# Converting float64 weights: exponents in a tile of their own, the mantissa in place

## The chip, the cores and the metric

The kernel runs on one core of a Trainium2 chip. The metric is the device time of one execution in microseconds (us): 1454.6, the median of three runs from 1453.09 to 1455.71. PE is TensorE, DVE is VectorE, ACT is ScalarE, POOL is GpSimd; SP, ACT and POOL also issue DMAs.

## The reference

Three steps in a row: an attention between tokens and 32 state rows for 8 batches of 8 heads, a mixture of 8 experts of which every token uses one, and a dense network on all 4352 tokens.

```python
xread = softmax(scale * x @ state.T) @ state      # per batch and head, D = 64
sread = softmax(scale * state @ x.T) @ x
x = concat(xread, sread)                          # 4352 tokens of 512
e = argmax(normalised x @ normalised expert_emb.T / tau)
x = gate * (relu(x @ w1[e]) @ w2[e])              # w1: 8 x 512 x 1024, w2: 8 x 1024 x 512
h = x @ w_in                                      # 512 x 2048
out = (h * clip(h + 3, 0, 6) / 6) @ w_out         # 2048 x 512
```

`w_in` and `w_out` come in as float64: their float32 draws are multiplied by a float64 number. The kernel sees them as pairs of 32-bit words.

## The kernel before

Products that need more precision than one pass gives are made from two parts: a weight or an activation is rounded to a high part (a cast), and a low part is the difference. PE then adds three products (high high, low high, high low).

The attention runs batch by batch. Its results go to DRAM, a routing stage sorts tokens into slots of 128 of one expert, and the slots are worked through in units: five leading slots of the largest expert, then pairs and single slots. An expert's weight pieces (128x512) are loaded to `raw` (L1231, L1234), cast to `wh` on ACT or DVE (L1245) and subtracted to `wl` on DVE or POOL (L1248); PE uses them at L1409 and L1450 (first product, `h_ps`) and L1512 (second product, `y_ps`). Beside the units, blocks of 256 sorted tokens go through the dense network: L1618 (`u_ps`, 12 matmuls for one of 16 pieces of `w_in`), L1622, L1625, L1629, L1632 (the activation and its two parts `gh`, `gl`), and L1653 (`o`, 6 matmuls for one of 16 pieces of `w_out`). The first block needs each of the 32 dense pieces for the first time.

A dense piece is 128x512 float64 numbers, 512 KB, loaded on ACT's queue (L259, L262) into a raw buffer. `Conv` turns it into float32 and then into two parts:

- `cs` (DVE): L271 takes the 11 exponent bits from the top 16 of each number and writes them over the lowest 16 bits; L272 takes the top 20 mantissa bits into a tile of its own, `cv_m`.
- `ct` (ACT): L276 turns the exponent into the bits of a bfloat16 power of two (in its place, the result a whole number of 16 bits); L277 turns the mantissa into 1 + m / 2^20.
- `cd` (DVE): L281 adds the sign bit; L282 adds 16 lower mantissa bits.
- `cp` (POOL or DVE, L286): mantissa times signed power. `ch` (ACT, L293): the high part. `cl` (POOL or DVE, L296): the low part.

The first 14 pieces are converted during the attention and the routing, with two raw buffers and two `cv_m`. The other 18 use as raw buffers the two tiles `yw` and `yh` that later hold tokens, one piece in each at a time, pieces alternating, and rows of a shared pool for `cv_m`.

The order on every engine is set at build time by a planner (`Sched`). Each operation has a cost per engine, an urgency, operations it depends on and buffers that it takes and gives back. The planner keeps an estimated clock for each engine and puts next the operation that can start earliest, corrected by its urgency; where two engines can do an operation it takes the one that ends sooner. A raw buffer (`hr`) is taken by the load and, before, given back by `cp`; the `cv_m` buffer (`hc`) by `cl`. The estimates only set the order: on the chip, engines wait for each other by semaphores.

Of the kernel before, what the change touches and what calls it, by code (L numbers as in the profile page):

```python
# [8 lines left out]
F32 = mybir.dt.float32  # L9
F32R = mybir.dt.float32r  # L10
BF16 = mybir.dt.bfloat16
I32 = mybir.dt.int32
# [8 lines left out]
class Ring:  # L21
    """The buffers of a tag: the times from which those that nothing holds are free."""
# [5 lines left out]
class Hold:  # L28
    """A buffer of a ring, from the operation that takes it to the last of those that read it."""
# [9 lines left out]
class Sched:  # L39
    """Puts operations in the order of the engines' queues: by an estimate of the engines' times, an engine that  # L40
    is free takes the most urgent of the operations whose operands and buffers are there."""
# [9 lines left out]
    def op(self, fn, cost, prio, deps=(), take=(), give=(), dma=0.0, after=None):  # L51
        """After deps have ended, and behind after in the same queue."""
# [18 lines left out]
    def gate(self):  # L71
        """An operation of no engine, that done() does."""
        o = self.op(None, {}, 0.0)
        self.avail.remove(o)
        self.n -= 1
        return o
# [55 lines left out]
def kernel(  # L132
# [33 lines left out]
    # the expert with the most tokens comes first and has at least NT / E of them: the first NL slots are its own  # L166
    NL = -(-NT // (E * 128))
    # behind them, NP pairs of slots of the same expert, that there are always
    NP = -(-(-(-NT // 128) - NL - E) // 2)
    # the slots from NU on are often empty  # L170
    NU = 37
# [9 lines left out]
    # what is kept until the leading slots are done  # L181
# [9 lines left out]
    # A row of xd has its columns (c q a) of 32 in quarters q, for transposes in blocks of 32, the logits behind them:  # L191
    # (q (g (i a) e)), c = 2 g + i, with the products of the heads of g as the second part.
    def quarters(t, g):
        """Columns and logits of g in rows."""
        v = t.rearrange("p (q g w) -> p g q w", q=4, g=2)[:, g]
        return v[:, :, 0:64].rearrange("p q (i a) -> p q i a", i=2), v[:, :, 64:66]
# [25 lines left out]
    # ring buffers  # L222
# [12 lines left out]
    # the attention's end, the leading slots' end, and the end of the slots that may be left out  # L235
# [8 lines left out]
    class Conv:  # L244
        """A piece of a dense weight, rounded to float32, as two float32r parts. A float64 weight comes as its bits:
        exponent and mantissa apart (cs, ct), then the signed power of two, as a bfloat16 in the place of the lowest
        bits, times the mantissa (cd, cp), then the parts (ch, cl)."""
# [16 lines left out]
        def cs(self, pool):  # L264
            self.ma = self.raw
            if self.wide:
                h = self.raw.bitcast(U16).rearrange("p (f w) -> p f w", w=4)
                self.ex, self.low, self.sign = h[:, :, 0], h[:, :, 1], h[:, :, 3]
                self.ma = pool()
                top = self.raw.rearrange("p (f w) -> p f w", w=2)[:, :, 1]  # L270
                DVE.tensor_scalar(self.ex, self.sign, 4, 0x7FF, op0=ALU.logical_shift_right, op1=ALU.bitwise_and)  # L271
                DVE.tensor_scalar(self.ma.bitcast(I32), top, 0xFFFFF, None, op0=ALU.bitwise_and)  # L272

        def ct(self):
            if self.wide:
                ACT.activation(self.ex, self.ex, AF.Relu, bias=ebias[:, 0:1], scale=2.0**7)  # L276
                ACT.activation(self.ma, self.ma.bitcast(I32), AF.Copy, bias=1.0, scale=2.0**-20)  # L277

        def cd(self):
            if self.wide:  # L280
                DVE.scalar_tensor_tensor(self.ex, self.sign, 0x8000, self.ex, op0=ALU.bitwise_and, op1=ALU.bitwise_or)  # L281
                DVE.scalar_tensor_tensor(self.ma, self.low, 2.0**-36, self.ma, op0=ALU.mult, op1=ALU.add)  # L282
# [18 lines left out]
    def convert(n, prio, pool, ma, gate=None, start=0.0):  # L301
        """Takes over a piece: into the buffers of pool, from gate on."""
# [6 lines left out]
        b = op(lambda: c.cs(ma), {"D": 0.67}, prio, [a], [hc])  # L309
        d = op(c.ct, {"A": 1.13}, prio, [b])  # L310
        e = op(c.cd, {"D": 1.2}, prio, [d])
        f = op(*((lambda: c.cp("P"), {"P": 1.225}) if early else (c.cp, {"D": 0.6, "P": 1.225})), prio, [e], (), [hr])
# [1556 lines left out]
```

## Time and profile before

| | |
|---|---|
| median of three runs | 1454.6 us |
| profiled execution, first to last instruction | 1453.4 us |
| PE busy | 1354.7 us, 93% |
| DVE busy | 917.8 us, 63% |
| ACT busy | 645.3 us, 44% |
| POOL busy | 543.1 us, 37% |

The profile tells of one execution. For it the page gives the span of 1453.4 us; the time of that execution from outside isn't given apart, and the runs' median is 1.2 us above the span. The share of busy time is a mean over stages: PE is nearly full from about 450 us on, and has gaps in the attention, the routing, and the stage after it, in which the leading slots end and the first dense block runs.

### The profile page before, as it was taken

Reading aid. Unit: us, or ns where it says so; the run is one execution under the profiler, and the core shown is the slowest. Engines: PE = TensorE matmul, PEld = TensorE weight load, DVE = VectorE, ACT = ScalarE, POOL = GpSimd, SP = SyncE. Lnnn points to the kernel's source line nnn. Section 1 sums busy time; section 2 is a strip of 40 time slices with the busy share of each in tenths; the row PEclk is TensorE's granted clock in tenths of the full one; section 3 lists DMA queues with packets and bytes.
Section 4 is the critical chain, followed back from the end, with each engine's and each line's share of the span. In section 5 each row is a group of like instructions: output and inputs, shape, how many; then the busy total and the mean of one; then the engine's idle time right before and its main releaser. Section 6 shows DMA issues by size and latency. Waiting matters only on the chain. (4 is left out here: it accounts for less than half of the span.)

```text
span 1453.4 us, 25243 instructions
## 1 busy us (share of the span) xinstructions
PE 1354.7 (93%) x8976; PEld 1199.0 (82%) x8976; DVE 917.8 (63%) x2008; ACT 645.3 (44%) x1347; POOL 543.1 (37%) x558
## 2 busy tenths in 40 slices
PE   7896697877799999999999999999999999999997
PEld 6675686766688898989989898999998999899996
DVE  6988888899976555645454544665666675433332
ACT  4785435555643343434444343555544444333332
POOL 5554448566555232524142322244344322200000
PEclk8996689899899999999999999999999999999999
DMA  6643435555564333423243333555455544201000
GB/s 162 175 160 116 148 96 161 156 188 159 157 182 149 94 115 89 136 82 124 90 125 98 108 104 100 154 150 177 152 148 153 174 139 140 74 23 30 15 16 15
DMA packets 151765, 175.64 MB, mean 121 GB/s; under 512 B 43784, under 2 KB 116488, under 8 KB 150608
## 3 DMA queue, kind: packets, MB, share of 16 engines
q1 hardware_dynamic: 128544, 121.19, 28.2%
q0 software_dynamic: 12336, 35.99, 8.2%
q10 hardware_dynamic: 10752, 16.78, 3.6%
q8 instruction: 73, 1.20, 0.4%
q14 instruction: 60, 0.49, 0.1%
HBM read 146.09 MB, written 27.82 MB: 120 GB/s over the span
## 5 line engine op out<-in xcount | busy, mean ns | idle before, releaser
L1618 PE MATMUL u_ps<-yh,wih 128*128 128x256 f32 x1088 | 306.9, 282 | 6.0 <-DVE gl L1632 4.3
L1618 PE MATMUL u_ps<-yh,wil 128*128 128x256 f32 x1088 | 306.8, 282 | 3.1 <-DVE wil L296 3.1
L1618 PE MATMUL u_ps<-yw,wih 128*128 128x256 f32 x1088 | 307.0, 282 | 0.0
L1248 POOL TENSOR_TENSOR wl<-raw,wh 128x512 fp32r<-128x512 f32 x129 | 176.6, 1373 | 274.4 <-ACT wh L1245 127.3
L1625 DVE SCALAR_TENSOR_TENSOR u_ps<-r,u_ps 128x256 f32<-128x256 f32 x272 | 116.2, 427 | 255.0 <-ACT r L1622 240.5
L1622 ACT ACTIVATE r<-u_ps,three 128x256 f32<-128x256 f32 x272 | 129.1, 475 | 305.4 <-PE u_ps L1618 277.2
L1618 PEld LDWEIGHTS u_ps<-yh,wih 128*128 128x128 f32 x1088 | 207.3, 191 | 17.2 <-DVE gl L1632 4.3
L1653 PE MATMUL o<-woh,gh 128*128 128x512 f32 x544 | 217.0, 399 | 2.0 <-DVE yo L1667 1.2
L1653 PE MATMUL o<-wol,gh 128*128 128x512 f32 x544 | 216.4, 398 | 0.0
L1653 PE MATMUL o<-woh,gl 128*128 128x512 f32 x544 | 214.9, 395 | 0.0
L1618 PEld LDWEIGHTS u_ps<-yw,wih 128*128 128x128 f32 x1088 | 206.6, 190 | 8.5
L1618 PEld LDWEIGHTS u_ps<-yh,wil 128*128 128x128 f32 x1088 | 207.5, 191 | 3.3 <-DVE wil L296 3.3
L1512 PE MATMUL y_ps<-wh,hx 128*128 128x512 f32 x512 | 186.3, 403 | 1.3 <-DVE wh L1245 1.3
L1629 ACT CAST gh<-u_ps 128x256 fp32r<-128x256 f32 x272 | 101.2, 372 | 187.9 <-PE o L1653 140.4
L1248 DVE TENSOR_TENSOR wl<-raw,wh 128x512 fp32r<-128x512 f32 x223 | 160.5, 727 | 33.4 <-ACT wh L1245 29.6
L1632 DVE TENSOR_TENSOR gl<-u_ps,gh 128x256 fp32r<-128x256 f32 x272 | 114.4, 421 | 98.0 <-ACT gh L1629 94.3
L1276 POOL DMA_INDIRECT xq<-xd,qidx x128 | 136.1, 1063 | 54.0 <-issue 31.9
L1245 ACT CAST wh<-raw 128x512 fp32r<-128x512 f32 x197 | 120.9, 619 | 73.3 <-PE y_ps L1512 39.8
L1409 PE MATMUL h_ps<-xt,wh 128*128 128x256 f32 x704 | 140.9, 288 | 3.8 <-ACT wh L1245 3.8
L1672 POOL DMA_INDIRECT out_dram<-yo,ix x34 | 35.9, 1057 | 273.3 <-ACT gh L1629 160.0
L1653 PEld LDWEIGHTS o<-woh,gl 128*128 128x128 f32 x544 | 102.6, 189 | 25.2
L1409 PEld LDWEIGHTS h_ps<-xt,wh 128*128 128x128 f32 x704 | 117.6, 197 | 5.7 <-ACT wh L1245 4.2
(312 smaller groups left out, 2474.2 us busy)
## 6 DMA issues: line engine op xcount, KB each, us to landing
raw<-in_moe_w_dram SPq DMA_DIRECT2D x176, 512.0 KB
yl<-ysd SPq DMA_DIRECT2D x136, 64.0 KB
xd<-xr SPq DMA_DIRECT2D x8, 1056.0 KB
ysd<-yt POOLq DMA_DIRECT2D x32, 256.5 KB
xb<-in_x_dram SPq DMA_DIRECT2D x48, 128.0 KB
yw<-in_moe_w_out_dram ACTq DMA_DIRECT2D x9, 512.0 KB
cv_raw<-in_moe_w_in_dram ACTq DMA_DIRECT2D x8, 512.0 KB
yh<-in_moe_w_in_dram ACTq DMA_DIRECT2D x8, 512.0 KB
```

The costliest lines, as they stand in the source:

```text
L1245: copy[e](pc["hi"], box["t"][:, j, :])
L1248: eng[e].tensor_tensor(pc["lo"], box["t"][:, j, :], f32(pc["hi"]), op=ALU.subtract)
L1276: POOL.indirect_dma_start(q[:, j * QW:(j + 1) * QW], None, xd_q, index(qidx[:, j, s:s + 1]))
L1409: PE.matmul(out(f), pc[w][:, (2 * c + f) * 128:(2 * c + f + 1) * 128], u.xt[a][:, 2 * j + c, 256 * hf:256 * hf + 256], start=new and c == ...
L1512: PE.matmul(u.y[i], u.ht[t][:, a, lo + 128 * i:lo + 128 * i + 128], pc[w], start=c == 0 and k == 0, stop=c == KF - 1 and k == 2)
L1618: PE.matmul(p, w, y[:, k, :], start=k == 0 and j == 0, stop=k == KD - 1 and j == 2)
L1622: ACT.activation(q["r"], q["p"], AF.Relu, bias=pool["three"][:, 0:1])
L1625: DVE.scalar_tensor_tensor(q["p"], q["r"], 6.0, q["p"], op0=ALU.min, op1=ALU.mult)
L1629: ACT.copy(q["h"], q["p"])
L1632: DVE.tensor_tensor(q["l"], q["p"], f32(q["h"]), op=ALU.subtract)
L1653: PE.matmul(o["o"][a], g[:, a * 128:(a + 1) * 128], w, start=m == 0 and j == 0, stop=m == KFF - 1 and j == 2)
L1672: POOL.indirect_dma_start(out, bass.IndirectOffsetOnAxis(ap=o["ix"][:, a:a + 1], axis=0), box["t"], None)
```

## The change

The exponents get the tile that the mantissa had (`cv_m`, now used as 512 16-bit numbers side by side), and the mantissa stays in the raw buffer: its mask, its conversion and the lower bits' addition are written in place, 32 bits at every second word. The mask moves from `cs` to `cd`; the conversion becomes a step of its own on ACT (`cu`), and the addition one on DVE (`cm`). So a piece goes DVE, ACT, DVE, ACT, DVE, then `cp`, `ch`, `cl`, where it went DVE, ACT, DVE, `cp`, `ch`, `cl`. The number of instructions of each kind is the same. The raw buffer is now given back by `cl`, and the `cv_m` tile by `cp`. The planner's costs of the steps are new, and with them its order on all engines. Lines move by up to 10: L1245 is L1255 after, L1248 is L1258, L1632 is L1642. The rest of the diff takes comments out.

```diff
         def cs(self, pool):
...
-                self.ex, self.low, self.sign = h[:, :, 0], h[:, :, 1], h[:, :, 3]
-                self.ma = pool()
-                top = self.raw.rearrange("p (f w) -> p f w", w=2)[:, :, 1]
+                self.low, self.sign = h[:, :, 1], h[:, :, 3]
+                self.top = self.raw.rearrange("p (f w) -> p f w", w=2)[:, :, 1]
+                self.ma = self.top.bitcast(F32)
+                self.ex = pool().bitcast(U16)[:, 0:512]
                 DVE.tensor_scalar(self.ex, self.sign, 4, 0x7FF, op0=ALU.logical_shift_right, op1=ALU.bitwise_and)
-                DVE.tensor_scalar(self.ma.bitcast(I32), top, 0xFFFFF, None, op0=ALU.bitwise_and)
         def ct(self):
             if self.wide:
                 ACT.activation(self.ex, self.ex, AF.Relu, bias=ebias[:, 0:1], scale=2.0**7)
-                ACT.activation(self.ma, self.ma.bitcast(I32), AF.Copy, bias=1.0, scale=2.0**-20)
         def cd(self):
             if self.wide:
                 DVE.scalar_tensor_tensor(self.ex, self.sign, 0x8000, self.ex, op0=ALU.bitwise_and, op1=ALU.bitwise_or)
+                DVE.tensor_scalar(self.top, self.top, 0xFFFFF, None, op0=ALU.bitwise_and)
+        def cu(self):
+            if self.wide:
+                ACT.activation(self.ma, self.top, AF.Copy, bias=1.0, scale=2.0**-20)
+        def cm(self):
+            if self.wide:
                 DVE.scalar_tensor_tensor(self.ma, self.low, 2.0**-36, self.ma, op0=ALU.mult, op1=ALU.add)
...
-        b = op(lambda: c.cs(ma), {"D": 0.67}, prio, [a], [hc])
-        d = op(c.ct, {"A": 1.13}, prio, [b])
+        b = op(lambda: c.cs(ma), {"D": 0.6}, prio, [a], [hc])
+        d = op(c.ct, {"A": 0.62}, prio, [b])
         e = op(c.cd, {"D": 1.2}, prio, [d])
-        f = op(*((lambda: c.cp("P"), {"P": 1.225}) if early else (c.cp, {"D": 0.6, "P": 1.225})), prio, [e], (), [hr])
+        e = op(c.cu, {"A": 0.68}, prio, [e])
+        e = op(c.cm, {"D": 0.72}, prio, [e])
+        f = op(*((lambda: c.cp("P"), {"P": 1.225}) if early else (c.cp, {"D": 0.6, "P": 1.225})), prio, [e], (), [hc])
         g = op(c.ch, {"A": 0.52}, prio, [f, home])
-        dense[conv_q[n]] = op(*((lambda: c.cl("P"), {"P": 1.225}) if early else (c.cl, {"D": 0.6, "P": 1.225})), prio, [g], (), [hc])
+        dense[conv_q[n]] = op(*((lambda: c.cl("P"), {"P": 1.225}) if early else (c.cl, {"D": 0.6, "P": 1.225})), prio, [g], (), [hr])
```

Three places show what moves. The first is DVE's order late among the 18 pieces, where one piece takes all its steps; before (L271 and L272 are `cs`, L281 and L282 `cd`, L286 `cp`; the `gl` and `u_ps` rows are the dense block's):

```order
L271 TENSOR_SCALAR yw_4025<-yw_4025 128x512
L272 TENSOR_SCALAR cv_m_4081<-yw_4025 128x512
L1632 TENSOR_TENSOR gl_4070<-u_ps_3965,gh_4069 128x256
L1248 TENSOR_TENSOR wl_4073<-raw_4008,wh_4072 128x512
L1625 SCALAR_TENSOR_TENSOR u_ps_4056<-r_4096,u_ps_4056 128x256
L281 SCALAR_TENSOR_TENSOR yw_4025<-yw_4025 128x512
L282 SCALAR_TENSOR_TENSOR cv_m_4081<-yw_4025,cv_m_4081 128x512
L1248 TENSOR_TENSOR wl_4117<-raw_4040,wh_4116 128x512
L286 TENSOR_TENSOR cv_m_4081<-cv_m_4081,yw_4025 128x512
```

And now (L273 is `cs`, L281 and L282 `cd`, L290 `cm`, L294 `cp`, L304 `cl`; `hx` belongs to a unit):

```order
L273 TENSOR_SCALAR cv_m_4099<-yw_4060 128x512
L304 TENSOR_TENSOR wil2_3177<-yh_3938,wih2_3176 128x512
L281 SCALAR_TENSOR_TENSOR cv_m_4099<-yw_4060,cv_m_4099 128x512
L282 TENSOR_SCALAR yw_4060<-yw_4060 128x512
L1442 SCALAR_TENSOR_TENSOR hx_4134<-h_ps_4046,hx_4134 128x512
L1442 SCALAR_TENSOR_TENSOR hx_4151<-h_ps_4102,hx_4151 128x512
L290 SCALAR_TENSOR_TENSOR yw_4060<-yw_4060 128x512
L294 TENSOR_TENSOR yw_4060<-yw_4060,cv_m_4099 128x512
L273 TENSOR_SCALAR cv_m_4166<-yh_4118 128x512
L304 TENSOR_TENSOR wol2_3175<-yw_4060,woh2_3174 128x512
```

The step `cm` stands between the mask and `cp`, with other work in front of it, a piece's last step stands one row behind the next piece's first, and the two `wl` are gone from DVE's stretch. Next, ACT's order among the same pieces, before (L262 and L259 are loads, L293 is `ch`):

```order
L262 DMA yw_3793<-in_moe2_w_out_dram 128x1024
L293 CAST woh2_3068<-cv_m_3708 128x512
L1354 ACTIVATE l8_3704,gates_83<-l8_3704,nr_3712 128x8
L259 DMA yh_3805<-in_moe2_w_in_dram 128x4x256
L293 CAST wih2_3070<-cv_m_3723 128x512
```

And now (L263 and L260 are the loads, L301 is `ch`):

```order
L301 CAST woh2_3174<-yw_3561 128x512
L301 CAST wih2_3176<-yh_3591 128x512
L1639 CAST gh_3772<-u_ps_3612 128x256
L1364 ACTIVATE l8_3647,gates_83<-l8_3647,nr_3668 128x8
L263 DMA yw_3777<-in_moe2_w_out_dram 128x1024
L260 DMA yh_3780<-in_moe2_w_in_dram 128x4x256
```

The next loads stood in front of the casts of the pieces before them, and stand behind them now. Last, POOL's order late among the 18 pieces, before (L1248 is a `wl`, L1270 a gather of tokens):

```order
L1248 TENSOR_TENSOR wl_4281<-raw_4159,wh_4280 128x512
L1248 TENSOR_TENSOR wl_4301<-raw_4159,wh_4300 128x512
L1248 TENSOR_TENSOR wl_4307<-raw_4230,wh_4306 128x512
L1248 TENSOR_TENSOR wl_4382<-raw_4230,wh_4381 128x512
L1270 DMA xg_4420<-xd_69,gidx1_79 128x528
L286 TENSOR_TENSOR cv_m_4386<-cv_m_4386,yw_4347 128x512
```

And now:

```order
L1258 TENSOR_TENSOR wl_4092<-raw_4041,wh_4091 128x512
L1258 TENSOR_TENSOR wl_4095<-raw_4041,wh_4094 128x512
L1258 TENSOR_TENSOR wl_4160<-raw_4089,wh_4159 128x512
L1258 TENSOR_TENSOR wl_4163<-raw_4089,wh_4162 128x512
L1258 TENSOR_TENSOR wl_4220<-raw_4149,wh_4219 128x512
L1258 TENSOR_TENSOR wl_4259<-raw_4149,wh_4258 128x512
L1258 TENSOR_TENSOR wl_4283<-raw_4203,wh_4282 128x512
L1258 TENSOR_TENSOR wl_4291<-raw_4203,wh_4290 128x512
```

POOL now makes the second parts of both halves of every load here, where DVE made some of them before.

## Rows read from the trace of the kernel before

**Rows 1.** The page: busy us, share of the span and instructions by engine.

```profile
PE 1354.7 (93%) x8976; PEld 1199.0 (82%) x8976; DVE 917.8 (63%) x2008; ACT 645.3 (44%) x1347; POOL 543.1 (37%) x558
```

**Rows 2.** Stretches: length; PE, PEld, DVE, ACT, POOL busy; granted clock; DMA share; GB/s.

```profile
60.00:160.00 100.00, 71.20 (x748) 58.59 (x748) 88.40 (x207) 62.22 (x99) 51.87 (x82) 0.79 0.50 163
...
260.00:410.00 150.00, 116.09 (x617) 99.04 (x618) 144.93 (x233) 85.36 (x155) 93.44 (x71) 0.89 0.53 162
...
450.00:1200.00 750.00, 748.93 (x4816) 676.25 (x4816) 427.01 (x992) 322.37 (x726) 261.51 (x248) 1.00 0.42 126
```

**Rows 3.** PE's waits, 260 to 410 us: total us, times, longest.

```profile
PE y_ps L1512 <- POOL wl L1248: 6.8, 3, 4.1
PE y_ps L1512 <- DVE wl L1248: 5.7, 3, 2.7
PE h_ps L1409 <- DVE wl L1248: 5.3, 2, 3.4
PE h_ps L1409 <- POOL wl L1248: 5.1, 5, 1.6
PE u_ps L1618 <- DVE gl L1632: 4.3, 3, 3.0
PE h_ps L1409 <- ACT wh L1245: 3.8, 2, 2.2
PE u_ps L1618 <- DVE wil L296: 3.1, 1, 3.1
PE u_ps L1618 <- ACT wih L293: 0.8, 1, 0.8
```

**Rows 4.** Tile cv_m: ns least/median/most, first and last start, form.

```profile
L277 ACT ACTIVATE cv_m<-cv_m x32: 629/687/706, 48.8 to 401.5; 128x512 f32<-128x512 int32 x32
...
L293 ACT CAST woh<-cv_m x16: 611/620/623, 208.0 to 404.8; 128x512 fp32r<-128x512 f32 x16
...
L272 DVE TENSOR_SCALAR cv_m<-yw x9: 428/464/3205, 265.6 to 390.2; 128x512 int32<-128x512 int32 x9
...
L282 DVE SCALAR_TENSOR_TENSOR cv_m<-yw,cv_m x9: 706/729/1717, 273.7 to 393.1; 128x512 f32<-128x512 uint16 x9
...
L296 DVE TENSOR_TENSOR wol<-cv_m,woh x9: 671/678/1508, 284.1 to 406.4; 128x512 fp32r<-128x512 f32 x9
...
L286 POOL TENSOR_TENSOR cv_m<-cv_m,yh x3: 1280/1282/1399, 277.6 to 340.2; 128x512 f32<-128x512 f32 x3
L286 DVE TENSOR_TENSOR cv_m<-cv_m,yw x3: 679/679/1773, 311.3 to 383.7; 128x512 f32<-128x512 f32 x3
```

**Rows 5.** Lines L271, L276, L281: the same columns.

```profile
L271 DVE TENSOR_SCALAR yw<-yw x9: 725/746/1839, 265.1 to 389.7; 128x512 uint16<-128x512 uint16 x9
...
L276 ACT ACTIVATE yw<-yw,ebias x9: 1424/1465/1495, 268.1 to 390.5; 128x512 uint16<-128x512 uint16 x9
...
L281 DVE SCALAR_TENSOR_TENSOR yw<-yw x9: 1302/1322/1374, 272.5 to 392.0; 128x512 uint16<-128x512 uint16 x9
```

**Rows 6.** Lines L1245 and L1248: the same columns.

```profile
L1245 DVE CAST wh<-raw x155: 383/427/1533, 212.0 to 1248.4; 128x512 fp32r<-128x512 f32 x155
...
L1248 DVE TENSOR_TENSOR wl<-raw,wh x223: 648/684/4239, 209.2 to 1249.2; 128x512 fp32r<-128x512 f32 x112
L1248 POOL TENSOR_TENSOR wl<-raw,wh x129: 1264/1292/2103, 162.1 to 1247.4; 128x512 fp32r<-128x512 f32 x129
```

**Rows 7.** Timeline, DVE and ACT: start us, length us; idle before it, releaser.

```profile
265.08 0.75 DVE L271 TENSOR_SCALAR yw<-yw 128x512 uint16<-128x512 uint16 x1
...
311.97 0.33 ACTq L262 DMA_DIRECT2D yw<-in_moe_w_out_dram  x1
...
317.48 0.76 DVE L271 TENSOR_SCALAR yw<-yw 128x512 uint16<-128x512 uint16 x1 [0.21 <-DMA yw<-in_moe_w_out_dram]
...
318.27 1.44 ACT L276 ACTIVATE yw<-yw,ebias 128x512 uint16<-128x512 uint16 x1 [2.18 <-DVE yw L271]
...
389.69 0.73 DVE L271 TENSOR_SCALAR yw<-yw 128x512 uint16<-128x512 uint16 x1
```

## The prediction

> **What bounds the kernel now.** I read the busy line first, then busy time and granted clock by stretch, then the waits of the tensor engine in the one stretch that matters, and last the conversion's own instructions. PE is busy 93% of the span [rows 1]; from 450 to 1200 us it is busy 748.9 of 750 us at a granted clock of 1.00 (2.4 GHz), and nothing gained on another engine there can show. The stretch from 260 to 410 us is different: PE has 116.1 busy us in 150 at a mean granted clock of 0.89, while DVE has 144.9, so DVE is idle for 5.1 us of it [rows 2]. PE's waits there add up to 34.9 us: 18.4 end with a DVE instruction (5.7 + 5.3 + 4.3 + 3.1), 11.9 with POOL's `wl`, 4.6 with ACT [rows 3]. So DVE sets the pace of this stretch, everything else queues behind it, and 18 of the 32 weight pieces are converted in it (nine in `yw`, nine in `yh`). The other 14 are converted in the attention before it, which is paced less clearly (60 to 160 us: DVE 88.4 of 100 us, PE 71.2 [rows 2]).
>
> **The change part by part.** A piece now costs DVE L271 0.746 us, L272 0.464, L281 1.322, L282 0.729 [rows 4, 5]: 3.26 us. All read every fourth 16-bit or every second 32-bit element, eight bytes apart. The two that also write at that step are the dear ones: L281 against L282, 1.322 against 0.729, both 512 elements of the same operation; L271 against L272, 0.746 against 0.464. On ACT it is the same: L276, reading and writing 16 bits at eight bytes, takes 1.465 us, L277 0.687.
> - The exponents are now written side by side. The first step (L271) then reads with a step and writes without, like L272: 0.464, at most the old 0.746. The sign step (L281) becomes like L282: 0.729, at most 1.322. Relu on ACT becomes like L277: 0.687, at most 1.465.
> - The mantissa is now written in place: 32 bits at eight bytes. No row of before writes so. From below the nearest rows are those of the same operations with plain writes: mask 0.464, `cu` 0.687, `cm` 0.729, `cp` 0.679 on DVE. From above they are the rows with 16-bit writes at that step: 0.746, 1.465, 1.322, 1.322. I take the lower end: reading 32 or 16 bits at this step costs almost nothing (L282 0.729 against L296 0.678), so the step by itself isn't dear, and the dear rows have one thing more in common, that an element is less than a word.
> - With these, DVE per piece is 0.464 + 0.729 + 0.464 + 0.729 = 2.39 us: 0.87 less, 15.7 us less over the 18 pieces. ACT saves 0.78 per piece, 14 us over the 18; ACT is busy 85.4 of 150 us, so this shortens the chain only.
> - The order changes. Up to the twentieth L1632 on DVE (the dense network's first block is past its last new weight there) DVE is given 10 fewer L1245 (29 to 19), 13 fewer L1248 (35 to 22) and 4 more `cp` (9 to 13). At 0.427, 0.684 and 0.679 [rows 4, 6] that is -4.3 - 8.9 + 2.7 = -10.5 us. POOL takes the 13 `wl` and gives back 4 `cp`: about 13 x 1.292 - 4 x 1.282 = +11.7 us on 93.4 of 150 [rows 2, 4, 6]. That is hidden as long as POOL isn't full.
> - The tensor engine's order puts 18 more L1512 in front of the first L1653, and 24 fewer L1618 and 12 fewer L1409 in front of the sixteenth. The latter 36 come later, where PE is full: one matmul there takes 748.9 / 4816 = 0.156 us [rows 2], so up to 5.6 us; the 18 take 2.8 in front. I book 4.3 us as lost.
> - One step more, and the raw buffer is held to the piece's last step. A buffer's round is now: load, all steps to the multiplication, next load. The nine pieces in `yw` begin from 265.08 to 389.69 us: eight rounds of 15.6 us. From the load's issue to the first step it takes 317.48 - 311.97 = 5.5 us [rows 7]. The new chain from there to the last step is, in order, 0.464 + 0.687 + 0.729 + 0.464 + 0.687 + 0.729 + 0.679 (1.282 on POOL) + 0.620 + 0.678: 5.7 to 6.4 us; with hand-overs of at most 0.1 us between engines, seven of them (L271 ends at 318.24, L276 starts at 318.27 [rows 7]), 6.4 to 7.1. So a round can't be shorter than 11.9 to 12.6 us. By DVE's work: 144.9 / 150 x 15.6 = 15.1 us in a round now, less (15.7 + 10.5) / 9 = 2.9: 12.2. The two bounds lie together, and queues never run without gaps, so I take 13.8 us: 1.8 less in each of nine rounds, 16.2 us.
>
> Sum: -16.2 + 4.3 - 2 (attention: 14 pieces save DVE 12 us there, but PE's waits are spread over many lines, so I count a sixth) = -13.9. The profiled execution's span of 1453.4 us is 1.2 below the median of the runs, 1454.6; I make the difference against the span and add it to the median: 1440.7, taken as 1440. The 18.4 us of waits that end with DVE hold the 13.9.
>
> The row says that reads at eight bytes run at nearly full speed (0.729 against 0.678). The Trainium skill (Vector Engine (DVE) Microarchitecture Reference, 5.2 Measured stream behaviour on trn2) says that a port keeps its rate only with runs of two or more adjacent words that start on an eight-byte boundary; for reads at this step the trace disagrees, and for 32-bit writes no run here shows it. By that rule the in-place writes would be dear, which is the first rival. The Trainium skill (SBUF — State Buffer, Door 1: The DMA port swizzle) speaks of lines of 16 bytes of which two hits are enough; by it the in-place writes would be free, and the reads in the trace agree.
>
> **The rivals.**
> *Writes at eight bytes are dear whatever their width.* For it: every such write in the trace is dear, on two engines. Against it: all of them are 16 bits wide. Then mask, `cu`, `cm` and `cp` take their upper ends: DVE per piece 0.464 + 0.729 + 0.746 + 1.322 = 3.26, nothing saved; 13 `cp` on DVE cost 0.643 more, 8.4 us, against the 10.5 of the order. ACT saves nothing. The chain grows to 0.464 + 0.687 + 0.729 + 0.746 + 1.465 + 1.322 + 1.322 + 0.620 + 0.678 = 8.0, a round with load and hand-overs is 14.2 at least, and with DVE as full as now about 16.2: 0.6 x 9 = 5.4, and 4.3 lost: 1464.
> *The held buffer decides.* The steps get cheaper, but the load of the next piece waits for the last step, which stands in two more queues than the step that now frees it. If that eats the gain, the round stays or grows to 16: 3.6 + 4.3 - 2 = +6, 1460. It turns slower where the round shrinks by less than 0.26 us (2.3 / 9). Against it: in the new order the last step stands one row behind the next piece's first.
> *The waits go to POOL.* DVE gets free, but the pieces' second parts wait on POOL (11.9 us of PE's waits now), which gets 11.7 us more: then the stretch keeps its length and 1455 comes out. Against it: POOL has 56.6 idle us there [rows 2].
>
> **How the numbers follow.** Forecast 0.58, with its own range 1427 to 1450 (round 12.4 to 15); dear writes 0.22; held buffer 0.12; POOL 0.08. No change is within 0.2%, 2.9 us, about what a measurement of this kernel can tell. Faster: 0.54 of the forecast, 0.06 of the others: 0.60. Same: 0.03 + 0.03 + 0.02 + 0.05 = 0.13. Slower: 0.27, nearly all from the first two rivals. The range reaches from 1424 (both bounds of a round met) to 1463, which leaves out about half of the dear writes.
>
> **What would show it.** Right: the sign step near 0.73, Relu near 0.69, mask near 0.46, `cu` near 0.69, `cm` near 0.73; the first steps in `yw` 13 to 14.5 us apart; DVE's busy time in the stretch down by 20 us or more; PE at 99% some 14 us earlier. Wrong: `cu` near 1.46 or `cm` near 1.3 (first rival); rounds of 15.6 us or more with DVE idle, waiting for a load (second); PE's waits for POOL's `wl` well over 12 us (third).

## The result, and the profile after

The changed kernel takes 1470.06 us (median of four runs, 1469.14 to 1471.68) against 1454.51 for the kernel before in the same job: a ratio of 1.0105, 95% interval 1.0091 to 1.012. It is slower by 15.5 us where some 14 us less was forecast, and lies outside the stated range.

The busy line of the page, which answers to [rows 1]:

```profile
PE 1359.6 (93%) x8976; PEld 1200.8 (82%) x8976; DVE 894.1 (61%) x1986; ACT 636.2 (43%) x1358; POOL 544.8 (37%) x569
```

The stretches of [rows 2], with the same columns:

```profile
60.00:160.00 100.00, 70.49 (x745) 56.70 (x744) 84.58 (x191) 57.62 (x99) 52.42 (x81) 0.81 0.48 154
260.00:410.00 150.00, 115.84 (x616) 97.23 (x617) 121.19 (x209) 76.96 (x154) 81.63 (x69) 0.89 0.50 155
450.00:1200.00 750.00, 748.58 (x4769) 675.53 (x4768) 426.64 (x988) 318.95 (x718) 270.65 (x256) 1.00 0.42 126
```

Between 260 and 410 us DVE is busy 23.7 us less than before, about as forecast, and PE no more than before (115.84 against 116.09). From 450 to 1200 us PE is as full as before, yet it gets 47 fewer matmuls through (4769 against 4816), so on average one takes longer.

The conversion's steps after, for the pieces in `yw` and in tile `cv_m` (ns least, median, most; first and last start; form), answering to [rows 4, 5]:

```profile
L277 ACT ACTIVATE cv_m<-cv_m,ebias x32: 706/722/761, 47.4 to 416.7; 128x512 uint16<-128x512 uint16 x32
L273 DVE TENSOR_SCALAR cv_m<-yw x9: 416/428/1415, 274.1 to 407.8; 128x512 uint16<-128x512 uint16 x9
L281 DVE SCALAR_TENSOR_TENSOR cv_m<-yw,cv_m x9: 677/691/731, 278.1 to 409.3; 128x512 uint16<-128x512 uint16 x9
L282 DVE TENSOR_SCALAR yw<-yw x9: 428/431/1407, 278.9 to 410.1; 128x512 int32<-128x512 int32 x9
L286 ACT ACTIVATE yw<-yw x9: 651/677/694, 281.0 to 410.5; 128x512 f32<-128x512 int32 x9
L290 DVE SCALAR_TENSOR_TENSOR yw<-yw x9: 651/682/1669, 282.2 to 412.8; 128x512 f32<-128x512 uint16 x9
```

On DVE these steps came out as priced or a little cheaper: 0.428 + 0.691 + 0.431 + 0.682 = 2.23 us for a piece (2.39 forecast, 3.26 before). On ACT Relu (L277) takes 0.722 us, 0.687 forecast. The 32-bit writes at every eight bytes cost nothing extra: 0.431, 0.677 and 0.682 us against 0.464, 0.687 and 0.729 for the plain writes of before [rows 4]. One step is dearer than its 0.679 us, the product where DVE does it (the same columns):

```profile
L294 DVE TENSOR_TENSOR yh<-yh,cv_m x9: 679/1353/6049, 284.6 to 421.5; 128x512 f32<-128x512 f32 x9
```

The shortest takes what it took before; the longest ran beside POOL, as the last section shows.

The line of L273 also holds the round that the forecast rests on: the first steps in `yw` go from 274.1 to 407.8, so eight rounds of 16.7 us, not 13.8 (before: 15.6). It shows a second thing: the first of these pieces begins 9.0 us later than before (265.08 [rows 7]). Its load is issued that much later, before and after (timeline: start, length):

```profile
259.17 0.33 ACTq L262 DMA_DIRECT2D yw<-in_moe_w_out_dram  x1
```

```profile
268.70 0.34 ACTq L263 DMA_DIRECT2D yw<-in_moe_w_out_dram  x1
```

What DVE waited for between 260 and 425 us, total, times, longest:

```profile
DVE cv_m L273 <- DMA yw<-in_moe_w_out_dram: 9.7, 6, 3.5
DVE hx L1442 <- ACT hx L1438: 4.9, 3, 2.9
DVE cv_m L273 <- DMA ysd<-yt: 4.2, 2, 2.9
DVE cv_m L281 <- ACT cv_m L277: 2.7, 8, 0.8
DVE cv_m L273 <- DMA yh<-in_moe_w_in_dram: 2.5, 3, 1.2
```

DVE, idle for 5.1 us of 150 before, now waits 12.2 us for the pieces' own loads: the sign that was named for the rival "the held buffer decides". PE's own waits from 260 to 410 us, which answer to [rows 3], the longest totals first:

```profile
PE h_ps L1419 <- POOL wl L1258: 7.8, 7, 3.8
PE u_ps L1628 <- DVE gl L1642: 7.3, 3, 4.9
PE h_ps L1419 <- DVE wl L1258: 4.3, 2, 3.6
PE u_ps L1628 <- ACT wih L301: 2.9, 1, 2.9
PE y_ps L1522 <- POOL wl L1258: 2.7, 2, 1.8
PE o L1663 <- DVE wol L304: 2.1, 2, 1.9
```

With the ten shorter rows that follow, 18.3 us end with a DVE instruction (18.4 before), 10.5 with POOL's `wl` (11.9 before) and 5.6 with ACT (4.6 before). DVE has 23.7 us less to do and is idle for 28.8 us of the 150, and PE waits for it as long as before.

How much is lost on the way is read at two places of the dense network's second product (L1653 before, L1663 after), each a pair of matmuls of high parts for one piece of `w_out`: the 24th such pair, in the second block, and the last one (count, ns, first to last start). Before:

```profile
L1653 PE MATMUL o<-woh,gh x2: 391/396/400, 477.4 to 478.1; 128*128 128x512 f32 x2
...
L1653 PE MATMUL o<-woh,gh x2: 398/399/400, 1443.6 to 1444.3; 128*128 128x512 f32 x2
```

After:

```profile
L1663 PE MATMUL o<-woh,gh x2: 391/396/400, 485.5 to 486.2; 128*128 128x512 f32 x2
...
L1663 PE MATMUL o<-woh,gh x2: 397/398/400, 1458.1 to 1458.8; 128*128 128x512 f32 x2
```

8.1 us are gone at the 24th pair, 14.5 at the last. So there are two losses: one before 480 us, and one of 6.4 us spread over the full part. The largest single wait of PE in the first is this (timeline: start, length, engine, line; idle before it and its releaser):

```profile
436.20 0.40 PE L1663 MATMUL o<-woh,gl 128*128 128x512 f32 x1
443.23 0.58 PE L1628 MATMUL u_ps<-yh,wih 128*128 128x256 f32 x1 [6.63 <-DVE gl L1642]
```

DVE is late with `gl` because that stands behind a gate step that waits for POOL. DVE's timeline has that step, and POOL's shows what it waits for queued behind the first block's two output writes:

```profile
440.99 0.15 DVE L1359 TENSOR_SCALAR nr<-nr 128x1 f32<-128x1 f32 x1 [7.31 <-POOL nr L1356]
```

```profile
434.98 1.01 POOL L1682 DMA_INDIRECT out_dram<-yo,ix  x1 [0.30 <-issue]
439.36 0.99 POOL L1682 DMA_INDIRECT out_dram<-yo,ix  x1 [3.37 <-issue]
440.37 1.11 POOL L1356 TENSOR_TENSOR nr<-nr,half 128x1 f32<-128x1 f32 x2
```

Before, the same step (L1346) runs at 415.62, ahead of the first output write (432.42), and PE's longest wait between 400 and 500 us is 2.7. So this wait comes from the order of POOL's queue.

### The profile page after: what moved, and what is told of

It is laid out like the page before. It is cut to its first block, busy times and chain, and to the rows that moved or that the text cites. A ratio compares the mean times of both kernels' runs of the same rounds, so it can differ in the third digit from the quotient of the medians.

```text
span 1468.0 us, 25211 instructions
## 1 busy us (share of the span) xinstructions
PE 1359.6 (93%) x8976; PEld 1200.8 (82%) x8976; DVE 894.1 (61%) x1986; ACT 636.2 (43%) x1358; POOL 544.8 (37%) x569
## 5 line engine op out<-in xcount | busy, mean ns | idle before, releaser
L1628 PE MATMUL u_ps<-yh,wih 128*128 128x256 f32 x1088 | 309.2, 284 | 19.7 <-DVE gl L1642 14.9
L1258 POOL TENSOR_TENSOR wl<-raw,wh 128x512 fp32r<-128x512 f32 x144 | 195.5, 1363 | 310.6 <-ACT wh L1255 166.4
L1628 PE MATMUL u_ps<-yh,wil 128*128 128x256 f32 x1088 | 308.9, 284 | 2.0 <-DVE wil L304 1.3
L1628 PE MATMUL u_ps<-yw,wih 128*128 128x256 f32 x1088 | 308.8, 284 | 0.3 <-DVE yw L1607 0.3
L1632 ACT ACTIVATE r<-u_ps,three 128x256 f32<-128x256 f32 x272 | 129.1, 475 | 306.6 <-PE u_ps L1628 280.4
L1628 PEld LDWEIGHTS u_ps<-yh,wih 128*128 128x128 f32 x1088 | 207.2, 190 | 32.0 <-DVE gl L1642 17.1
L1663 PE MATMUL o<-wol,gh 128*128 128x512 f32 x544 | 215.8, 397 | 2.1 <-DVE wol L304 2.1
L1663 PE MATMUL o<-woh,gh 128*128 128x512 f32 x544 | 215.5, 396 | 1.1 <-ACT woh L301 0.6
L1663 PE MATMUL o<-woh,gl 128*128 128x512 f32 x544 | 215.4, 396 | 0.6 <-DVE gl L1642 0.6
L1628 PEld LDWEIGHTS u_ps<-yw,wih 128*128 128x128 f32 x1088 | 207.3, 191 | 9.3 <-DVE yw L1607 0.9
L1628 PEld LDWEIGHTS u_ps<-yh,wil 128*128 128x128 f32 x1088 | 208.1, 191 | 2.5 <-DVE wil L304 1.6
L1642 DVE TENSOR_TENSOR gl<-u_ps,gh 128x256 fp32r<-128x256 f32 x272 | 114.7, 422 | 101.9 <-ACT gh L1639 100.0
L1258 DVE TENSOR_TENSOR wl<-raw,wh 128x512 fp32r<-128x512 f32 x208 | 150.2, 730 | 33.5 <-ACT wh L1255 29.7
L1255 ACT CAST wh<-raw 128x512 fp32r<-128x512 f32 x206 | 125.9, 619 | 73.7 <-PE y_ps L1522 39.2
L1286 POOL DMA_INDIRECT xq<-xd,qidx x128 | 130.8, 1022 | 51.7 <-issue 33.1
L1663 PEld LDWEIGHTS o<-woh,gl 128*128 128x128 f32 x544 | 102.2, 188 | 24.8 <-DVE gl L1642 1.0
```

What stands on the lines that cost most here:

```text
L1255: copy[e](pc["hi"], box["t"][:, j, :])
L1258: eng[e].tensor_tensor(pc["lo"], box["t"][:, j, :], f32(pc["hi"]), op=ALU.subtract)
L1286: POOL.indirect_dma_start(q[:, j * QW:(j + 1) * QW], None, xd_q, index(qidx[:, j, s:s + 1]))
L1628: PE.matmul(p, w, y[:, k, :], start=k == 0 and j == 0, stop=k == KD - 1 and j == 2)
L1632: ACT.activation(q["r"], q["p"], AF.Relu, bias=pool["three"][:, 0:1])
L1642: DVE.tensor_tensor(q["l"], q["p"], f32(q["h"]), op=ALU.subtract)
```

## Experiments

The theories: **A**, the longer hold of the raw buffer; **B**, the added step and the changed order; **C**, the place of `yw` and `yh` in memory (the index tile `ix` was allocated in front of them before and behind them after, so they lie 96 bytes lower); **D**, POOL's second parts `wl` set the pace; **S**, the kernel before has a lucky order and nearly any other would cost it some 10 us; **N**, a small change of the order moves the time by little. Each run is compared with the kernel before measured beside it, in the same job (1454.8 to 1455.9).

### Where yw and yh lie

```diff
+ pool["ix0"] = [pool["ffn"].tile([128, 2], I32, tag="ix", name="ix", bufs=3)]   # in open_main
- o["ix"] = pool["ffn"].tile(...)
+ o["ix"] = pool["ix0"].pop() if i == 0 else pool["ffn"].tile(...)
```

This is the changed kernel; the kernel before got the counterpart, its first `yw` and `yh` taken in `open_main`. Every engine's order stays, row for row.

> The changed kernel with every instruction in its place; only the small index tile stands in front of yh and yw, which moves these 96 bytes up, to where the kernel before has them. Theory C (the place of yh and yw sets the spacing of u's matmuls): spacing 117 ns instead of 119.7, the 24th pair near 485 as now, and the time 5 to 6.5 us less, 1463.5 to 1465. Rival (the spacing differs for another reason, such as the run): 119.7 ns and 1470.

> The kernel before with every instruction in its place; only yh and yw lie 96 bytes lower, where the changed kernel has them. Theory C: spacing of u's matmuls 119.7 ns instead of 117.3, nothing else, and 1460 to 1461. Rival: 117.3 ns and 1454.5.

Measured: 1462.82 (ratio 1.0052, 1.0039 to 1.0066) for the changed kernel with the tiles moved back, 1459.89 (1.0035, 1.0023 to 1.0047) for the kernel before with them moved down. PE busy by line L1618 or L1628 alone, 500 to 1400 us (length; PE busy and count; PEld; clock, DMA share, GB/s), in turn before, before moved, after, after moved back:

```profile
500.00:1400.00 900.00, 355.18 (x2712) 346.45 (x2713) 1.00 0.37 110
```

```profile
500.00:1400.00 900.00, 359.26 (x2700) 349.57 (x2700) 1.00 0.36 110
```

```profile
500.00:1400.00 900.00, 355.86 (x2674) 345.87 (x2673) 1.00 0.36 110
```

```profile
500.00:1400.00 900.00, 352.15 (x2688) 343.31 (x2689) 1.00 0.37 110
```

Busy time over count is 131.0, 133.1, 133.1 and 131.0 ns for one matmul: the address alone makes 2.1 ns. (It holds the tail of the last of every twelve matmuls, so it is more than the 117 to 120 ns from start to start that the expectations speak of.) The page counts 3 x 1088 of them, so 6.8 us; measured are 7.2 one way, or 8.1 with each time taken against the kernel before in its own job (15.5 - 7.4), and 4.5 the other. Both times lie a little under the expected ranges, and theory C is shown in both directions.

```diff
- o["ix"] = pool["ffn"].tile([128, 2], I32, tag="ix", name="ix", bufs=3)
+ o["ix"] = pool["ix0"].pop() if i == 0 else pool["ffn"].tile([128, 2], I32, tag="ix" if i % 3 else "ixa", name="ix", bufs=2 if i % 3 else 1)
```

Here one index tile of 32 bytes is taken in front (`ixa`, a buffer of its own), where the run above took all three, 96 bytes.

> The changed kernel in its order, with yh and yw 32 bytes higher (207776 and 215968) instead of 96 (207840 and 216032). If what counts is that the buffers start at a multiple of 64 bytes (207744 and 215936 do, the others don't): spacing of u's matmuls 117 to 118 ns and 1463. If it takes the whole 96 bytes: 119.7 ns and 1470.

Measured, one run:

```profile
500.00:1400.00 900.00, 353.34 (x2688) 343.83 (x2688) 1.00 0.37 111
```

That is 131.5 ns for one matmul, and the time is 1467.3. The spacing agrees with the idea that a start at a multiple of 64 bytes is what costs, from three places alone; the time fell less than expected, and one run can't tell why.

### The dear writes put back

```diff
- self.ex = pool().bitcast(U16)[:, 0:512]
+ self.ex = h[:, :, 0]
```

> The changed kernel in its order, hold and addresses, but with the exponents left in the raw tile's 16-bit places at eight bytes as before (the first, Relu and the sign step dear again, the mantissa in place). Theory A (the round of a held buffer paces the conversion): every piece's chain grows by about 0.3 + 0.75 + 0.65 = 1.7 us, the first steps in a buffer lie about 18.4 us apart instead of 16.7, last of them 13 us later, the 24th pair near 495 and the time near 1480. Theory B (the pace comes from the order and not from the length of a piece's chain): 1470 to 1473.

Measured: 1491.46 (1.025, 1.0237 to 1.0264), the 24th pair at 504.5. The first steps lie 18.3 us apart:

```profile
L273 DVE TENSOR_SCALAR yw<-yw x9: 739/754/1860, 277.5 to 423.6; 128x512 uint16<-128x512 uint16 x9
```

The three steps with 16-bit writes are as dear as before the change (0.754, Relu 1.462, sign 1.327), and the mask in `yw`, left as it was, takes 1.176 instead of 0.431. In one and the same order the rounds grow by 1.6 us and the end comes 21 us later, more than a longer chain alone was expected to cost. It is no measure of the gain, since an order made for cheap steps can hurt dear ones more than their own order does.

### The raw buffer free from the product on

The exponents go to the second half of the piece's tile and the product to the whole of it, so the raw buffer is given back by `cp`, as before the change:

```diff
- self.ex = pool().bitcast(U16)[:, 0:512]
+ self.out = pool(); self.ex = self.out.bitcast(U16)[:, 512:1024]
...
- eng[e].tensor_tensor(self.ma, self.ma, self.ex.bitcast(BF16), op=ALU.mult)
+ eng[e].tensor_tensor(self.out, self.ma, self.ex.bitcast(BF16), op=ALU.mult); self.ma = self.out
```

> The changed kernel, but the product of mantissa and exponent goes to the piece's own tile (exponents in its second half), so a raw buffer is free from the product on and not from the last step on. Theory A (what is lost before 480 us is the longer hold of the raw buffer): the early loads of the attention stand near 142 to 229 us again instead of 172 to 245, the first pair of the dense network's second products starts near 274 instead of 285, the 24th near 477 or earlier instead of 485.5, the first steps in one buffer lie 13.5 to 15 us apart instead of 16.7, and the time falls by 8 us or more, to 1462 or less. Theory B (the additional step and the changed order cost it): the stretch keeps its length, rounds 16 or more, 24th pair 484 or later, time 1464 or more. The tiles yh and yw lie at other addresses than in the changed kernel, as in the kernel before; theory C (their place sets the spacing of u's matmuls) wants 117 ns here instead of 119.7, worth 6 us, so A and C together give about 1450 to 1456.

> Only the 14 pieces converted in the attention give their raw buffer back at the product; the 18 later ones hold it to the last step, as in the changed kernel. yh and yw stand where the kernel before has them, so it is compared with 1462.8 (all held) and 1456.1 (none held). If the hold costs mainly by the six early pieces of the second weight, that wait for the attention's end with their raw buffers in hand: 1456 to 1458, first steps in a later buffer still 16 us or more apart. If it costs by the rounds of the later buffers: 1461 to 1463.

Measured: 1456.12 (1.0011, 1.0001 to 1.002) free everywhere, 1455.81 (0.9999, 0.9986 to 1.0013) free for the early pieces alone. The early loads of `w_out` came back by little: free everywhere they are issued from 169.6 to 240.2 us (before 141.7 to 229.4, after 172.2 to 245.4), so that part of theory A fell.

```profile
L263 ACTq DMA_DIRECT2D cv_raw<-in_moe_w_out_dram x6: 334/334/399, 169.6 to 240.2; - x6
```

The rounds say more. The first steps in `yw`, free everywhere and then free early alone:

```profile
L273 DVE TENSOR_SCALAR cv_m<-yw x9: 409/428/3121, 268.8 to 388.4; 128x512 uint16<-128x512 uint16 x9
```

```profile
L273 DVE TENSOR_SCALAR cv_m<-yw x9: 417/428/2186, 268.7 to 395.4; 128x512 uint16<-128x512 uint16 x9
```

Rounds of 14.95 and of 15.8 us (119.6 and 126.7 over eight): the last piece starts 7 us sooner in one than in the other, and the two kernels take the same time. By its expectation the second run speaks for the hold of the early pieces as what costs, but its order differs too, so the two are not separated. From one order to another the end does not follow the round of a raw buffer; within one order it does, as the dear writes showed. Free everywhere, the 24th pair starts at 473.8, as early as expected and 3.6 us sooner than before, and the last at 1442.8, only 0.8 sooner.

```profile
L1663 PE MATMUL o<-woh,gh x2: 391/396/400, 473.8 to 474.5; 128*128 128x512 f32 x2
```

With the dear writes in the run that frees the buffer everywhere (the exponents again in `h[:, :, 0]`, its order unchanged):

> The run with the raw buffer free from the product on, in its order and at its addresses, but with the exponents left in the raw tile's 16-bit places: each piece has about 0.96 us more on DVE and 0.75 on ACT. Theory A (DVE and a piece's chain still set the pace, so the cheaper steps are worth their time): 1456 + 10 to 18, 1466 to 1474, and 24th pair near 486 instead of 473.8. Theory D (with the buffer free early, the pace comes from the expert weights' second parts on POOL and the ring they fill, and the cheaper steps are worth little): 1456 to 1460.

Measured: 1482.19 (1.0179, 1.0161 to 1.0198), 26 us above 1456.1, more than theory A wanted and far from D. So the cheap steps are worth a lot in the order made for them, and still the kernel is no faster than before. That the new order costs what they give is the reading tested below.

### The split of the second parts

One number told to the planner, or three, moves `wl` between POOL and DVE. The first is changed in the run that frees the buffer everywhere, and in the kernel before:

```diff
- pc["op"] = op(lo, {"D": 0.6, "P": 1.225}, prio[j], [a], (), [hr])
+ pc["op"] = op(lo, {"D": 0.6, "P": 1.8}, prio[j], [a], (), [hr])
```

> The run with the raw buffer free from the product on, but with the planner told that the second part of an expert weight takes POOL 1.8 us instead of 1.225, so that it gives about 43 of POOL's 153 of these to DVE, which has some 25 idle us between 300 and 450. yh and yw stand where the kernel before has them. Theory D (POOL's second parts set the pace of the stretch): the tensor engine's waits for them between 230 and 450 us fall from 18.2 to under 10, and the time to 1446 to 1452, faster than both kernels. Theory A (DVE sets the pace) or a mere scatter of orders: 1455 to 1462.

> The kernel before with the same cost of 1.8 us told to the planner, which moves about 35 second parts of expert weights from POOL to DVE. The prediction held that DVE sets the pace of the stretch from 260 to 410 us in the kernel before: then each of them there costs about 0.68 us of it, some 10 of them 5 to 8 us, 1459 to 1463. Theory D (POOL sets it in the kernel before too): 1446 to 1452.

The change tells the planner 2.52 us of DVE for a piece's first steps, where they take 2.23; before, it was told 1.87, where they take 3.26. So the next edit lowers the numbers in the run that frees the buffer (cut to the three costs):

```diff
- cs: {"D": 0.6}    cd: {"D": 1.2}    cm: {"D": 0.72}
+ cs: {"D": 0.45}   cd: {"D": 0.9}    cm: {"D": 0.52}
```

And in the kernel before they are raised, `cs` from 0.67 to 0.9 and `cd` from 1.2 to 1.62:

> The run with the raw buffer free from the product on, but the planner is told as much DVE time for a piece's first steps as in the kernel before (0.45 + 0.90 + 0.52 = 1.87 us instead of 2.52). It then leaves 29 of the expert weights' second parts on DVE up to the 20th L1642 instead of 22 (the kernel before: 35). yh and yw have the addresses of the kernel before, with the names exchanged. If the gain of the steps was given away because the planner was told that DVE has more to do while it has less, and so filled POOL: 1448 to 1452, as with 30 of them by the other way (1450.0). If that run was fast by chance of its order: 1455 to 1460.

> The kernel before, steps and places unchanged, with the planner told 2.52 us of DVE for a piece's first steps instead of 1.87, as the changed kernel tells it: 24 second parts on DVE up to the 20th L1632 instead of 35. By the prediction (DVE sets the pace there, POOL has room) it gets faster: 10 fewer of 0.68 us, 1447 to 1452. If POOL's second parts bind as soon as it gets more of them: 1456 to 1463.

Both together in the run that frees the buffer:

> The run with the smaller DVE times told to the planner and, besides, 1.8 us for a second part on POOL: 35 of them on DVE up to the 20th L1642, as many as in the kernel before. If POOL's second parts are what keeps the stretch long, it is as fast as the best so far or faster: 1444 to 1450. If DVE binds again at that number: 1452 to 1458.

Measured: 1450.05 (0.996, 0.9945 to 0.9974) for the first and 1450.08 (0.9964, 0.995 to 0.9978) for both together: these two beat both kernels. The smaller DVE times alone gave 1456.92 (1.0016, 1.0006 to 1.0026), in the range that was expected if 1450.05 was a chance of its order: the number of `wl` on DVE by itself is not the cause, nor did PE's waits for POOL's `wl` fall as wanted (18.2 to 15.1 us between 230 and 450 us in the run of 1450.05). The kernel before got slower both ways: by 10.5 us with 250 instead of 223 `wl` on DVE in all (1466.38; 1.0069, 1.0054 to 1.0084; above both expected ranges), and by 12.1 us with 213 (1467.12; 1.0073, 1.0053 to 1.0093). Up to the 20th L1632 the first has 36 of them on DVE against 35, so what it shows is another order, and not the price of a `wl` on DVE in the stretch. The second is the plainest answer to the prediction: with the steps of before, 11 `wl` and 6 `wh` are taken off DVE up to the 20th L1632 (by the change 13 and 10). Its stretch from 260 to 410 us, then PE's three longest waits in it, by total:

```profile
260.00:410.00 150.00, 115.37 (x602) 99.19 (x600) 141.00 (x209) 81.61 (x145) 98.16 (x75) 0.85 0.53 160
```

```profile
PE h_ps L1409 <- POOL wl L1248: 9.8, 4, 4.1
PE y_ps L1512 <- POOL wl L1248: 8.7, 3, 4.4
PE o L1653 <- DVE gl L1632: 7.2, 2, 4.2
```

PE's waits for POOL rise from 11.9 us [rows 3] to 18.5, and DVE, relieved of 24 instructions, is busy only 3.9 us less [rows 2].

### Any other order

That the kernel before loses 10 to 12 us in both directions suggested theory S: its order is a lucky one. The test changes only a piece's due time, by 0.5 us either way, in three kernels that all have `yw` and `yh` at the old addresses: the steps of before, the changed steps with the hold to the last step, and the changed steps with the buffer free at the product.

```diff
- convert(n, conv_use[conv_q[n]] - 36.654,
+ convert(n, conv_use[conv_q[n]] - 36.154,
```

> The kernel before with nothing changed but the due time of a piece in the planner, 0.5 us later (36.154 instead of 36.654): the steps, their costs and their places stay, the order of about a tenth of the rows moves. Theory S (the order of the kernel before is a lucky one, and nearly any other costs it some 10 us, as the two runs of it with another split of the second parts did, 1466.4 and 1467.1): 1460 to 1470. Theory N (a small change of the order moves the time by little, and those two were slow because of the second parts that they moved): 1453 to 1458.

> The same with the due time 0.5 us earlier (37.154). Theory S: 1460 to 1470. Theory N: 1453 to 1458.

> The run with the cheap steps and the raw buffer free from the product on (1456.1), with a piece's due time 0.5 us later. Theory S: its order is already any order, so another one gives about the same, 1453 to 1459, some 10 us under the kernel before in any other order: that would be the gain of the cheaper steps. Theory N: the same numbers here, but then the two runs of the kernel before stay at 1453 to 1458 as well, and the cheaper steps have gained nothing.

> The same with the due time 0.5 us earlier (37.154). Theory S and theory N: 1452 to 1460; under 1450 or over 1465 would say that the order scatters by as much here as it does in the kernel before.

> The changed kernel's steps and its hold to the last step, yh and yw at the addresses of the kernel before (as the run of 1462.8), with a piece's due time 0.5 us later in the planner. If the hold itself costs 6 to 7 us against the runs that free the buffer at the product (1453.2 to 1456.9 in five orders): 1459 to 1465 here too. If 1462.8 was one bad order: 1453 to 1458.

> The same with the due time 0.5 us earlier. If the hold costs: 1459 to 1465. If 1462.8 was one bad order: 1453 to 1458.

| | own due time | 0.5 us later | 0.5 us sooner | mean of the two |
|---|---|---|---|---|
| steps of before | 1454.8 | 1460.44 (1.0035, 1.0022 to 1.0048) | 1465.57 (1.0073, 1.0056 to 1.0089) | 1463.0 |
| changed steps, held | 1462.8 | 1458.0 (1.0014, 1.0001 to 1.0027) | 1458.59 (1.0028, 1.0018 to 1.0037) | 1458.3 |
| changed steps, free at the product | 1456.1 | 1455.95 (1.0003, 0.9994 to 1.0013) | 1453.2 (0.9988, 0.9974 to 1.0002) | 1454.6 |

Theory S holds for the kernel before as far as it was tried: all four other orders are 5.6 to 12.1 us slower than its own. With the hold, the own order is the slowest of three, so 1462.8 may in part be one bad order; 1458.0 and 1458.59 lie at the end of the range expected for that case (1453 to 1458) and just above it. Shifted alike, the changed steps are faster than those of before, by 2.4 and 7.0 us with the hold and by 4.5 and 12.4 without; at the own due time they are slower, by 8.0 and 1.3. Over all three due times the means are 1460.3, 1459.8 and 1455.1.

Taking in the runs with other splits as well, the four other orders of the steps of before took 1460.4 to 1467.1, the three with the hold 1458.0 to 1462.8, and six with the buffer free everywhere 1450.1 to 1456.9. So without the hold the cheaper steps show in every order tried, against any order of the kernel before but its own; with the hold the difference is not told apart from the scatter of orders.

## Why the prediction was wrong, point by point

**The steps' cost: right.** The writes at eight bytes that are dear have elements of 16 bits, as I took it; 32-bit writes at the same step cost nothing extra. The first rival is out. The mechanism behind it, as the Trainium skill (Vector Engine (DVE) Microarchitecture Reference, 5.2 Measured stream behaviour on trn2) has it, that a write stream wants adjacent pairs, would have made L282 and L290 dear, and the trace disagrees: 0.431 and 0.682.

**The step that failed: the round and its nine-fold gain.** I took a round of 13.8 us and booked 1.8 x 9 = 16.2 us at the end of the kernel. The round grew to 16.7, DVE waiting for loads, as the second rival had it (it priced that at 1460; at the old addresses 1462.8 came). And the first piece, whose start I took as given, began 9.0 us later. Under the round lies the premise that DVE sets the pace of the stretch. Its busy time fell by 23.7 us, about as forecast (26.2), and PE's waits that end with DVE, which were to hold the whole gain, stayed at 18.3 us against 18.4. At the largest single wait, the 6.6 us for `gl`, what DVE stood behind in its queue counted, and not how full it was.

The size of the round was not the only fault. Rounds of 14.95 and 15.8 us in two orders gave 1456.1 and 1455.8, so from order to order the end does not follow it, and it is doubtful that a round shortened as forecast would have given 16.2 us. In the sum itself the gain is booked nine times where there are eight rounds from the first piece to the last (14.4 us), and the 4.3 us lost are not worked out from their two parts, 5.6 and 2.8. Shifted alike, the hold costs 2.0 and 5.4 us, and 6.7 at the own due time: a size, from three pairs of orders, and no more.

**The order: priced by counting, wrong in sign.** I added up the moved instructions (-10.5 us on DVE, +11.7 hidden on POOL, 4.3 lost). With nothing but a move of that kind the kernel before became 12 us slower. A planner's order has a value of its own: the kernel before is 8.2 us faster than the mean of its two neighbours (1463.0 - 1454.8), and the changed kernel with the hold 4.5 slower than the mean of its own (1462.8 - 1458.3). PE's wait behind a gate step in POOL's queue does not explain the 4.5: it is 7.1 us in the run of 1462.8, and 6.8 behind the same step in the run of 1458.59. Which waits make up either number stays open.

**The full part: put at nothing.** From 450 us on I held that nothing gained on another engine could show, and had no term for a matmul that itself gets longer. The changed order of allocation moved `yw` and `yh` by 96 bytes, and every L1628 became 2.1 ns longer: 7.2 us. Nothing in the diff or in the orders that I compared shows an address.

**The attention: the 2 us gained do not show.** From 60 to 160 us DVE is busy 84.58 us instead of 88.40, and PE 70.49 instead of 71.20: the freed DVE time bought nothing. The six early loads of `w_out` came 6 to 30 us later than before, and the first load into `yw` 9.5 us.

Put together along one path, from the kernel before to its two neighbours, to the held steps' two neighbours, to their own order, to the address: +8.2 - 4.7 + 4.5 + 7.2 = 15.2 of the 15.5 us. That the sum fits is no proof, since each step begins where the last one ended. The address is the one term that was measured with every order kept. The others are differences of means over two orders, up to 5 us apart, so -4.7 is not told apart from nothing. A gain of the kind forecast is shown for the version without hold against other orders of the kernel before (8.4 us in these means), and not for the changed kernel as it is.

The third rival, "the waits go to POOL", does not fit the changed kernel: PE's waits for POOL's `wl` are 10.5 us there from 260 to 410, not well over 12. It fits the version without hold by its time (1455 forecast, 1456.1 measured), where these waits are 18.2 us between 230 and 450 us (11.9 in the kernel before). It is part of the picture and not the whole: the run with smaller DVE times has 17.3 and is no faster, and the one of 1450.05 still has 15.1.

## What to carry to other kernels

Where a planner writes the queues, a change of its costs buys another order as well, and the order that a kernel comes with may be one of its best: compare a change with the kernel before in several orders (a due time shifted by half a microsecond both ways), and retune before you judge. Price a shortened loop of buffers only after asking which wait of the bound engine ends with it: an engine that is nearly full need not be what that engine waits for. And compare the addresses of the buffers that the full engine reads, since they can move without a line of the diff that says so.

## What the runs showed of the hardware

- **An operand's address is worth 1.6% of a matmul.** A float32r matmul with 256 columns from `yh` or `yw` is 131.0 ns apart from the next at 207840 and 216032 (32 bytes past a multiple of 64), and 133.1 at 207744 and 215936 (multiples of 64). At 207776 and 215968 it is 131.5, in one run. These are busy time over count, as above. Why, is open.
- **16-bit writes at eight-byte steps are slow on both engines**: for 512 elements 0.746 against 0.428 us (shift and mask), 1.322 against 0.691 (sign), 1.465 against 0.722 (Relu), where the reads kept their step or were packed as well.
- **An operation on DVE can stop while POOL works.** In the changed kernel one `cp` on DVE takes 6.05 us instead of 0.68, while POOL runs four operations; timelines of DVE and POOL from 284.4 us:

```profile
284.58 6.05 DVE L294 TENSOR_TENSOR yh<-yh,cv_m 128x512 f32<-128x512 f32 x1
290.55 0.42 DVE L1635 SCALAR_TENSOR_TENSOR u_ps<-r,u_ps 128x256 f32<-128x256 f32 x1
```

```profile
283.99 1.16 POOL L1286 DMA_INDIRECT xq<-xd,qidx  x1 [0.30 <-issue]
285.15 1.31 POOL L1258 TENSOR_TENSOR wl<-raw,wh 128x512 fp32r<-128x512 f32 x1
286.40 1.19 POOL L294 TENSOR_TENSOR yw<-yw,cv_m 128x512 f32<-128x512 f32 x1
287.54 2.53 POOL L1258 TENSOR_TENSOR wl<-raw,wh 128x512 fp32r<-128x512 f32 x2
```

The Trainium skill (SBUF — State Buffer, Who interferes with whom) says that a DVE instruction with two inputs in SBUF and a POOL instruction that reads SBUF exclude each other, and the one that comes second is blocked. The trace agrees that they exclude each other, and shows that DVE can lose four times in a row; which came first it does not settle, since `cp` starts before the first of the four, during a DMA that POOL issues. Over DVE's instructions that start between 260 and 450 us, what each took beyond the lower quartile of its kind, where that is over 0.25 us, adds up to 38.9 us before, 36.4 after and 48.4 in the run with 11 `wl` moved to POOL. All of these ran beside POOL, and a third or more of the sum is in instructions with one input, casts and the shift of L271 among them. So DVE's busy time holds such waiting, and in that run DVE with 24 instructions fewer from 260 to 410 us was busy only 3.9 us less.
